# A first convolution block in 64x32 tiles, eight at once, with the large band assembled by transfers inside SBUF

## The chip, the core and the metric

The kernel runs on one core of a Trainium2 chip. The metric is the device time of one execution in microseconds; the lower, the better. The median of three runs of the kernel before is 762.4 us (761.5 to 762.61).

## The reference: what is computed

A light-weight causal convolution along the sequence, followed by a gated feed-forward layer. `x` is (8, 4096, 192), the eight heads have 24 channels each, and each head has seven taps that go through a softmax first.

```
w   = exp(weight - max); w = w / (sum(w) + 1e-9)          # weight: 8 heads x 7 taps
y   = sum over k of w[h,k] * x_pad[b, s+k, channels of h]  # six zero rows ahead of each sequence
out = (relu(y @ w_gate) * (y @ w_val)) @ w_out             # 192 -> 1536 -> 192, 32768 rows
```

## The kernel before, in words

The 32768 rows are handled as two streams of four sequences each (`st` 0 and 1), in windows of 512 rows; two windows of both streams make a unit, and there are 16 units. Engines run side by side, each with its own list of instructions in order; ACT, SP and POOL also issue DMAs, and a queue whose next DMA must wait issues nothing that stands behind it.

*The opening* (units of work before the first gate/value matmul). PE can convolve by multiplying a block of x (rows on partitions) by a band matrix: column t of head h's band holds the seven weights in rows t to t+6. The opening makes this band from the eight softmaxes and convolves the first window with it, in these steps:

- PE runs warm-up matmuls (L193), spreads the raw taps over 128 partitions (L203), and clears three PSUM regions with the matmuls of L209.
- DVE takes the maximum `mx` (L275), ACT the exponential `e` (L278) and its sum (L281), DVE makes the blocks of the band (`prod` L287, `blk` L294, `sm` L295, `blocks` L299). POOL makes `wn`, the normalised taps, from `sm` (L308).
- PE shifts the blocks into place with `Z`, a matrix of ones in one diagonal stripe: eight shifts of 16 columns for each of three groups of heads, 24 matmuls (L335). DVE casts the three results to float16 (L343): `bands`, 118 rows by 112 columns per head.
- The first window of x is loaded as five overlapping pieces `jj` (up to 118 rows, both streams side by side, 384 columns of float32, tiles `prod1` to `prod5`) by SP (pieces 0, 3, 4) and ACT (pieces 1, 2), L109, and cast to float16 by ACT (L119). `STEPS0` sets the order 1, 0, 2, 3, 4.
- `conv_steps` convolves piece by piece in 112x32 tiles of the array: four at a time, each 32 channels of one stream, 106 columns (L391). The result's three parts of channels (`c`) lie in three PSUM tiles and are cast to `xc` by ACT and DVE (L402).

*Then* `gate_val` runs the gate and value matmuls (L621) for 12 groups `f` of 128 hidden channels, ACT applies the relu (L632), DVE multiplies (L633). The second window is convolved in the same way with `conv_steps` between groups 9 and 10 (`CONV1`), the third with `conv`. All later windows are convolved outside PE, on ACT, DVE and POOL (the lanes; they use `tap`, 20 small transfers on SP, L354). The weights Wg and Wv are loaded in four portions by POOL (L224) and copied to the second half of the partitions by DVE, POOL and SP (L231). L643 projects.

The order of work is the order of the code on each engine. A DMA issued by SP or ACT counts its completion on one of eight counters (`DMAHW0` to `DMAHW7`), taken in turn over both queues. A transfer that takes a counter again waits until that counter's last transfer has landed. Counters of POOL's transfers are called `DMASW`.

Of the kernel before, what the change touches and what calls it, by code (L numbers as in the profile page):

```python
# [9 lines left out]
F16 = mybir.dt.float16  # L10
# [5 lines left out]
def kernel(  # L16
# [50 lines left out]
    const = ctx.enter_context(tc.tile_pool(name="const", bufs=1))  # L67
# [30 lines left out]
        return xt  # L98

    xts = {0: staged(0, 0).rearrange("p (j s d) -> p j s d", s=2, d=D)}  # L100
    ROWS = [SUB + PAD, 112, 112, 112, 96]
    raw = [
        apool.tile([128, 2 * LPOOL], FP, name=f"prod{jj + 1}")[:, 0 : 2 * D] for jj in range(GSUB)
    ]

    def load_raw(queue, jj):
        lo = STEP * jj - PAD
        p0 = max(0, -lo)
        queue.dma_start(  # L109
            out=raw[jj][p0 : ROWS[jj], :].rearrange("p (s d) -> p s d", s=2),  # L110
            in_=bass.AP(
                tensor=x.tensor,
                offset=x.offset + (lo + p0) * D,
                ap=[[D, ROWS[jj] - p0], [NB * S * D, 2], [1, D]],
            ),
        )

    def cast(copy, jj):
        copy(  # L119
            out=xts[0][0 : ROWS[jj], jj, :, :].rearrange("p s d -> p (s d)"),  # L120
            in_=raw[jj][0 : ROWS[jj], :],
        )

    HR = 128 // H
    BW = HR + PAD
# [1 line left out]
    nc.scalar.activation(out=early[:], in_=nc.const_aps.tensor(0.0, [128, 1], FP), func=ACTF.Exp)  # L127
    w8 = const.tile([H, KW], FP)
    nc.sync.dma_start(out=w8[:], in_=weight)
# [5 lines left out]
    nc.vector.memset(zeros[:], 0.0)  # L135
    e = const.tile([128, KW + 1], FP)
    nc.vector.memset(e[:, KW:], 1e-9)

    ones = const.tile([128, 128], FP)
    nc.gpsimd.memset(ones[:], 1.0)  # L140
# [16 lines left out]
    Z = const.tile([128, 256], F16)  # L157
# [3 lines left out]
    with nc.allow_low_precision("one of the terms is not zero"):  # L161
        nc.vector.tensor_reduce(
            out=Z[:, 112 : 112 + HR],
            in_=eye[:].rearrange("p (g i) -> p i g", i=HR),
            axis=mybir.AxisListType.X,
            op=ALU.add,
        )
# [37 lines left out]
    BANDS = [range(0, 3), range(3, 6), range(6, H)]  # L205
    raised = [psum.tile([128, 2, 512], FP, name="ps") for _ in range(2)]
    raised = [raised[0][:, 0, :], raised[1][:, 0, :], held[:, 1, :]]
    for part, heads in zip(raised, BANDS):
        nc.tensor.matmul(  # L209
            out=part[:, 0 : SUB * len(heads)],  # L210
            lhsT=zeros[:],
            rhs=none(len(heads), SUB),
            start=True,
            stop=False,
            skip_group_check=True,
        )
# [54 lines left out]
    for s in range(2):  # L271
# [4 lines left out]
        out=mx[:], in_=spread[:, 0, 0:KW], axis=mybir.AxisListType.X, op=ALU.max, negate=True  # L276
# [5 lines left out]
    for jj in STEPS0[:3]:  # L282
# [5 lines left out]
        out=prod[:],  # L288
# [8 lines left out]
    for heads in BANDS:  # L297
        n = len(heads)
        nc.vector.scalar_tensor_tensor(  # L299
            out=blocks[:, heads[0] : heads[0] + n, :],  # L300
# [8 lines left out]
        out=wn[:], in0=e[:, 0:KW], scalar1=sm[:], scalar2=None, op0=ALU.mult  # L309
# [17 lines left out]
    bands = [const.tile([128, len(heads), SUB], F16, name=f"band{heads[0]}") for heads in BANDS]  # L327
    for part, heads, to, copy in zip(
        raised, BANDS, bands, [nc.vector.tensor_copy] * 3
    ):  # L330
        n = len(heads)
        for j in range(128 // HR):
            s0 = HR * j - PAD
            lo, hi = max(0, -s0), min(BW, SUB - s0)
            nc.tensor.matmul(  # L335
                out=part[:, 0 : SUB * n].rearrange("p (h t) -> p h t", t=SUB)[:, :, s0 + lo : s0 + hi],
                lhsT=Z[:, 112 - HR * j : 240 - HR * j],
                rhs=blocks[:, heads[0] : heads[0] + n, lo:hi],
                start=False,
                stop=(j == 128 // HR - 1),  # L340
                skip_group_check=True,
            )
        copy(out=to[:].rearrange("p h t -> p (h t)"), in_=part[:, 0 : SUB * n])  # L343

    tap = const.tile([128, NCH, KW], FP)

    for c in range(NCH):
        r0 = 0
        while r0 < 64:
            h = (64 * c + r0) // G  # L350
            r1 = min(64, G * (h + 1) - 64 * c)
            row = wn[HR * h : HR * h + 8, :]
            for st in range(2):
                nc.sync.dma_start(  # L354
                    out=tap[64 * st + r0 : 64 * st + r1, c, :],
                    in_=bass.AP(
                        tensor=row.tensor,
                        offset=row.offset,
                        ap=[row.ap[0], [0, (r1 - r0) // 8], [1, KW]],
                    ),  # L360
# [4 lines left out]
            both_halves(nc.sync.dma_start, 10, Wv)  # L365

    def band(h):
        return bands[h // 3][0 : SUB + PAD, h % 3, :]

    dense, xcs = {}, {}  # L370

# [5 lines left out]
    def conv_steps(g, ps, c, steps):  # L377


        for jj in steps:  # L380
            col = STEP * jj
            n = min(STEP, WIN - col)
            rows = n + PAD
            for second in range(2):
                for st in range(2):
                    for k2 in range(2):
                        k = 2 * c + k2
                        h0, h1 = 32 * k // G, (32 * k + 31) // G
                        h, m = (h0, G * h1 - 32 * k) if second else (h1, 32)
                        p0 = 64 * st + 32 * k2  # L390
                        nc.tensor.matmul(  # L391
                            out=ps[p0 : p0 + m, 0, col : col + n],
                            lhsT=xts[g][0:rows, jj, st, 32 * k : 32 * k + m],
                            rhs=band(h)[0:rows, 0:n],
                            start=True,
                            stop=True,
                            tile_position=(0, p0),
                            skip_group_check=True,
                        )

    def evict(copy, g, ps, c):
        copy(out=dense[0][:, g, c, :], in_=ps[:, 0, :])  # L402

    def conv(g):

# [303 lines left out]
    first = [psum.tile([128, 2, 512], FP, name="ps") for _ in range(NCH)]  # L709
    for c, steps in (  # L710
        (0, STEPS0[:3]), (1, STEPS0[:3]), (0, STEPS0[3:4]), (1, STEPS0[3:4]), (0, STEPS0[4:]), (1, STEPS0[4:]), (2, STEPS0)
    ):
        conv_steps(0, first[c], c, steps)
    both_halves(nc.vector.tensor_copy, 0, Wg)
    both_halves(nc.vector.tensor_copy, 0, Wv)
    for c, copy in enumerate((nc.scalar.copy, nc.vector.tensor_copy, nc.scalar.copy)):
        evict(copy, 0, first[c], c)
# [85 lines left out]
```

## Time and profile before

| | |
|---|---|
| median of three runs | 762.4 us |
| the profiled execution, its own time | 762.03 us |
| its span, first to last instruction | 760.3 us |
| PE busy | 756.3 us (99%) |
| DVE, ACT, POOL busy | 675.5 us, 610.0 us, 461.5 us |
| first gate/value matmul starts | 7.98 us |

A row of the timeline has start, duration, engine and line, the operation with its tile names, the number of instructions merged into the row, and in brackets the idle time of that engine before the row and what ended it. `SPq`, `ACTq` and `POOLq` are the queues as they issue DMAs. "x120" means 120 instructions merged; their starts overlap, so the duration is that of the whole row. A row of the chain of work that ended last has start, duration and what.

### The profile page before, as it was taken

Reading aid. Unit: us, or ns where it says so; the run is one execution under the profiler, and the core shown is the slowest. Engines: PE = TensorE matmul, PEld = TensorE weight load, DVE = VectorE, ACT = ScalarE, POOL = GpSimd, SP = SyncE. Lnnn points to the kernel's source line nnn. Section 1 sums busy time; section 2 is a strip of 40 time slices with the busy share of each in tenths; the row PEclk is TensorE's granted clock in tenths of the full one; section 3 lists DMA queues with packets and bytes.
Section 4 is the critical chain, followed back from the end, with each engine's and each line's share of the span. In section 5 each row is a group of like instructions: output and inputs, shape, how many; then the busy total and the mean of one; then the engine's idle time right before and its main releaser. Section 6 shows DMA issues by size and latency. Waiting matters only on the chain.

```text
span 760.3 us, 30529 instructions
## 1 busy us (share of the span) xinstructions
PE 756.3 (99%) x13723; PEld 457.7 (60%) x13723; DVE 675.5 (89%) x647; ACT 610.0 (80%) x680; POOL 461.5 (61%) x311
## 2 busy tenths in 40 slices
PE   9999999999999999999999999999999999999998
PEld 5555555566666666666666666666666666666658
DVE  7889989998998989989999899998999989897891
ACT  7897887878878788887877878788797887877671
POOL 8729649195591946829377392874919659193600
PEclk9999999999999999999999999999999999999999
DMA  9953532345324443334434324352233532240302
GB/s 142 139 66 91 80 85 46 43 96 75 85 44 52 98 66 85 54 62 83 60 85 71 66 67 55 85 85 73 52 49 93 77 86 44 23 100 9 85 2 85
DMA packets 153714, 54.07 MB, mean 71 GB/s; under 512 B 148912, under 2 KB 153584, under 8 KB 153584
## 3 DMA queue, kind: packets, MB, share of 16 engines
q1 hardware_dynamic: 117152, 37.61, 21.8%
q0 software_dynamic: 35808, 14.07, 16.3%
q8 instruction: 107, 1.75, 1.0%
q10 hardware_dynamic: 624, 0.44, 0.2%
q14 instruction: 23, 0.19, 0.1%
HBM read 28.98 MB, written 25.17 MB: 71 GB/s over the span
## 4 chain that ended last, share of the span: by engine, by line
PE 99%; DVE 0%; ACT 0%; issue 0%
PE ps L621 65%; PE ps L643 31%; PE ps L686 2%; PE ps L391 0%; PE ps L193 0%; PE ps L335 0%; PE ps L414 0%; ACT xc L402 0%; PE ps L203 0%; DVE prod L287 0%; ACT out_s L697 0%; DVE blk L294 0%; DVE blocks L299 0%; ACT e L278 0%; DVE mx L275 0%
## 5 line engine op out<-in xcount | busy, mean ns | idle before, releaser
L633 DVE TENSOR_TENSOR hT<-gr,ps 128x1024 f16<-128x1024 f16 (+1 forms) x385 | 468.9, 1218 | 35.8 <-ACT gr L632 8.7
L632 ACT ACTIVATE gr<-ps 128x1024 f16<-128x1024 f32 (+1 forms) x385 | 392.8, 1021 | 114.7 <-PE ps L621 114.6
L550 POOL TENSOR_TENSOR prod<-prod,prod 128x896 f32<-128x896 f32 x145 | 302.8, 2088 | 251.3 <-DVE prod L584 242.2
L621 PE MATMUL ps<-xc,Wg 64*64 64x512 f16 (+1 forms) x4464 | 318.6, 376 | 0.2 <-ACT xc L402 0.2
L621 PE MATMUL ps<-xc,Wv 64*64 64x512 f16 (+1 forms) x4464 | 318.6, 376 | 0.0
L643 PE MATMUL ps<-hT,Wo 64*64 64x512 f16 x4320 | 235.8, 376 | 0.0
L621 PEld LDWEIGHTS <-Wv 64*64 64x64 f16 (+1 forms) x4464 | 150.0, 106 | 98.7 <-DVE hT L633 0.3
L621 PEld LDWEIGHTS <-Wg 64*64 64x64 f16 (+1 forms) x4464 | 146.6, 107 | 102.0
L643 PEld LDWEIGHTS <-Wo 64*64 64x64 f16 x4320 | 138.5, 107 | 94.4
L538 ACT ACTIVATE prod<-x_r,tap 128x1024 f32<-128x1024 f16 (+2 forms) x195 | 182.7, 1017 | 0.0
L574 DVE SCALAR_TENSOR_TENSOR acc<-x_r,tap,acc 128x1024 f32<-128x1024 f16 (+3 forms) x150 | 118.0, 853 | 0.0
L661 DVE STREAM_TRANSPOSE out_s<-ps 128x1024 f32<-128x1024 f32 x45 | 56.1, 1248 | 28.4 <-PE ps L643 24.4
L550 POOL TENSOR_TENSOR xc<-prod,prod 128x896 f16<-128x896 f32 x29 | 60.7, 2092 | 2.3
L479 POOL COPY x_p<-x_e 128x1536 f16<-128x1536 f16 (+1 forms) x32 | 42.2, 1349 | 0.0
L251 POOL DMA_DIRECT2D x_e<-in_x_dram x30 | 26.6, 890 | 0.0
L574 DVE SCALAR_TENSOR_TENSOR xc<-x_r,tap,acc 128x1024 f16<-128x1024 f16 (+3 forms) x30 | 25.2, 839 | 0.0
L563 ACT ACTIVATE acc<-x_r,tap 128x1024 f32<-128x1024 f16 (+3 forms) x30 | 22.5, 801 | 0.0
L656 ACT COPY turned_by<-ps 128x2 f32<-128x2 f32 x45 | 7.0, 154 | 16.8 <-PE ps L643 14.8
L686 PEld LDWEIGHTS <-hT 128*128 128x128 f16 x192 | 15.8, 98 | 0.4 <-issue 0.4
L686 PE MATMUL ps<-Wo,hT 128*128 128x192 f16 x192 | 16.0, 246 | 0.0
L697 ACT COPY out_s<-ps 128x768 f32<-128x768 f32 (+2 forms) x5 | 3.2, 638 | 12.7 <-PE ps L686 12.7
L697 DVE COPY out_s<-ps 128x192 f32<-128x192 f32 x1 | 0.4, 357 | 13.3 <-PE ps L686 13.3
(61 smaller groups left out, 74.6 us busy)
## 6 DMA issues: line engine op xcount, KB each, us to landing
out_dram<-out_s SPq DMA_DIRECT2D x125, 192.0 KB
x_e<-in_x_dram POOLq DMA_DIRECT2D x28, 384.0 KB, 5.8
x_r<-x_p SPq DMA_TRANSPOSE x116
prod<-in_moe_w_out_dram POOLq DMA_DIRECT2D x1, 576.0 KB, 9.1
out_dram<-out_s SPq DMA_DIRECT2D x5, 96.0 KB
out_s<-in_x_dram POOLq DMA_DIRECT2D x2, 210.0 KB, 6.2
out_s<-in_x_dram POOLq DMA_DIRECT2D x2, 192.0 KB, 6.6
x_e<-in_x_dram POOLq DMA_DIRECT2D x2, 192.0 KB, 3.8
```

Of the source, the lines that this page charges most:

```text
L251: nc.gpsimd.dma_start(out=xe[:, 0:n, st, :, :].rearrange("p j c r -> p j (c r)"), in_=bass.AP(tensor=x.tensor, offset=x.offset + row * D, ...
L479: nc.gpsimd.tensor_copy(out=xp[:, js, :, st, :], in_=xe[:, js, st, :, :])
L538: nc.scalar.activation(out=both(prods[b, k], b, at, n), in_=shifted(b, c, k, t, n), func=ACTF.Copy, scale=tap[:, c, k : k + 1],)
L550: nc.gpsimd.tensor_tensor(out=acc if k < KW - 1 else xcs[b][:, w, :, :].rearrange("p c t -> p (c t)")[:, LDVE : NCH * WIN], in0=acc, in1=p ...
L563: nc.scalar.activation(out=both(accs[b], b, at, n), in_=shifted(b, c, 0, t, n), func=ACTF.Copy, scale=tap[:, c, 0:1],)
L574: nc.vector.scalar_tensor_tensor(out=result(b, at, n) if k == KW - 1 else both(acc, b, at, n), in0=shifted(b, c, k, t, n), scalar=tap[:, c ...
L621: nc.tensor.matmul(out=pss[i][q : q + M, st, :], lhsT=W[64 * st : 64 * st + 64, c, 128 * f + q : 128 * f + q + M], rhs=xcb[64 * st : 64 * ...
L632: nc.scalar.activation(out=gr[:, sts], in_=pss[0][:, sts], func=ACTF.Relu)
L633: nc.vector.tensor_tensor(out=h[:, f, sts], in0=gr[:, sts], in1=pss[1][:, sts], op=ALU.mult)
L643: nc.tensor.matmul(out=ps[64 * st : 64 * st + 64, b, :], lhsT=Wo[64 * r : 64 * r + 64, f, p, :], rhs=hs[b][64 * r : 64 * r + 64, f, st, :] ...
L661: nc.vector.transpose(out=o[:].rearrange("p t (b d) -> p b t d", b=2)[:, :, :, 32 * p : 32 * p + 32], in_=ps[:].rearrange("p b (t c) -> p ...
L686: nc.tensor.matmul(out=ps[:, i // 2, D * (i % 2) : D * (i % 2) + D], lhsT=h[:, f, st, 128 * q : 128 * (q + 1)], rhs=Wo[:, f, :, :].rearran ...
```

## The change

The first window, and it alone, is convolved in another way. It is seen as two halves of 256 rows, half `r` on partitions 64r to 64r+63, and each half as five pieces of 58 rows (the last 24) with six rows ahead. A band of only 64 rows by 58 columns, `near`, is made; since `Z` now has its stripe twice, 64 columns apart, the matmuls put the same band on partitions 0 to 63 and 64 to 127. The shifts number four for each group of heads, 12 in all. `conv_halves` works in 64x32 tiles: eight matmuls of 58 columns, two row halves by four column positions, each half in its own PSUM bank.

The second and third window still need the large band, `large`, 118 rows by 112 columns. It is cleared by DVE and filled by two transfers on SP, which lay `near` into it twice along the diagonal.

Each of the five loads of x becomes two (rows of half 0, rows of half 1): ten loads of 64 rows, but 58 in the first half of piece 0, where six rows of padding are not loaded, and 32 and 30 in piece 4. The casts of pieces 3 and 4 are divided: stream 0 on ACT, stream 1 on DVE.

```diff
+    HALF = WIN // 2
+    PIECE = 58
...
-    ROWS = [SUB + PAD, 112, 112, 112, 96]
+    LAST = 64 + HALF - PIECE * (GSUB - 1) + PAD
+    ROWS = [64 + PIECE + PAD] * (GSUB - 1) + [LAST]
...
-    def load_raw(queue, jj):
-        lo = STEP * jj - PAD
+    def load_raw(queue, jj, r):
+        lo = HALF * r + PIECE * jj - PAD
         p0 = max(0, -lo)
+        n = min(64, -(-(ROWS[jj] - 64) // 32) * 32) if r == 0 else ROWS[jj] - 64
         queue.dma_start(
-            out=raw[jj][p0 : ROWS[jj], :].rearrange("p (s d) -> p s d", s=2),
+            out=raw[jj][64 * r + p0 : 64 * r + n, :].rearrange("p (s d) -> p s d", s=2),
...
-    for queue, steps in ((nc.scalar, (1, 2)), (nc.sync, (0, 3, 4))):
-        for jj in steps:
-            load_raw(queue, jj)
+    for queue, pieces in (
+        (nc.scalar, ((1, 0), (1, 1), (2, 0), (2, 1))),
+        (nc.sync, ((0, 0), (0, 1), (3, 0), (3, 1), (4, 0), (4, 1))),
+    ):
+        for jj, r in pieces:
+            load_raw(queue, jj, r)
...
+    large = const.tile([128, H, SUB], F16, name="large")
+    nc.vector.memset(large[:], 0.0)
+    nc.vector.memset(raw[GSUB - 1][32:64, :], 0.0)
...
+    nc.vector.tensor_copy(out=Z[:, 176 : 176 + HR], in_=Z[:, 112 : 112 + HR])
...
     for jj in STEPS0[3:]:
-        cast(nc.scalar.copy, jj)
+        cast(nc.scalar.copy, jj, slice(0, 1))
...
-        for j in range(128 // HR):
+        for j in range(64 // HR):
...
+    for jj in STEPS0[3:]:
+        cast(nc.vector.tensor_copy, jj, slice(1, 2))
+
+    for t in range(0, SUB, PIECE):
+        n = min(PIECE, SUB - t)
+        nc.sync.dma_start(out=large[t : t + n + PAD, :, t : t + n], in_=near[0 : n + PAD, :, 0:n])
...
+    def conv_halves(g, ps, c, pieces):
+        for jj in pieces:
+            col = PIECE * jj
+            n = min(PIECE, HALF - col)
+            rows = n + PAD
...
+                        for r in range(2):
+                            nc.tensor.matmul(
+                                out=ps[p0 : p0 + m, r, col : col + n],
+                                lhsT=xts[g][64 * r : 64 * r + rows, jj, st, 32 * k : 32 * k + m],
+                                rhs=near[64 * r : 64 * r + rows, h, 0:n],
+                                start=True,
+                                stop=True,
+                                tile_position=(64 * r, p0),
+                                skip_group_check=True,
+                            )
```

How this stands in the engines' lists. On ACT, from the first load of x to the third cast, before (`prod2` is the tile of piece 1, `prod1` of piece 0, `prod3` of piece 2):

```order
L109 DMA prod2_87<-in_x_dram 112x2x192
L109 DMA prod3_88<-in_x_dram 112x2x192
L278 ACTIVATE e_102<-ps_121,mx_138 128x7 [waits DVE_49]
L281 ACTIVATE total_142,sm_141<-e_102 128x8 [waits Activation_49]
L119 CAST out_s_84<-prod2_87 112x384 [waits DMAHW3_49]
L119 CAST out_s_84<-prod1_86 118x384 [waits DMAHW1_49,Pool_49]
L119 CAST out_s_84<-prod3_88 112x384 [waits DMAHW5_49]
```

and now:

```order
L113 DMA prod2_87<-in_x_dram 64x2x192 x2
L113 DMA prod3_88<-in_x_dram 64x2x192
L113 DMA prod3_88<-in_x_dram 64x2x192 [waits DMAHW1_49]
L289 ACTIVATE e_107<-ps_130,mx_147 128x7 [waits DVE_49]
L292 ACTIVATE total_151,sm_150<-e_107 128x8 [waits Activation_49]
L123 CAST out_s_84<-prod2_87 128x384 [waits DMAHW5_49,DMAHW3_49]
L123 CAST out_s_84<-prod1_86 128x384 [waits DMAHW2_49,Pool_49]
L123 CAST out_s_84<-prod3_88 128x384 [waits DMAHW7_49,DMAHW1_49]
```

There are two loads more ahead of `e`, and the second of them, which is the upper half of piece 2, carries a wait for counter 1. On SP the same place, up to the first `tap` transfer, before:

```order
L129 DMA w8_93<-in_weight_dram 8x7
L109 DMA prod1_86<-in_x_dram 112x2x192
L109 DMA prod4_89<-in_x_dram 112x2x192
L109 DMA prod5_90<-in_x_dram 96x2x192
L354 DMA tap_217<-wn_156 24x1x7 [waits Pool_49]
```

and now:

```order
L133 DMA w8_93<-in_weight_dram 8x7
L113 DMA prod1_86<-in_x_dram 58x2x192
L113 DMA prod1_86<-in_x_dram 64x2x192
L113 DMA prod4_89<-in_x_dram 64x2x192 x2
L113 DMA prod5_90<-in_x_dram 32x2x192 [waits DMAHW0_49]
L113 DMA prod5_90<-in_x_dram 30x2x192 [waits DMAHW2_49]
L360 DMA large_109<-near_196 64x8x58 [waits DMAHW3_49,DVE_49]
L360 DMA large_109<-near_196 60x8x54 [waits DMAHW4_49]
L371 DMA tap_216<-wn_165 24x1x7 [waits DMAHW5_49,Pool_49]
```

Eleven transfers are now issued on the two queues before the large band's, so the counters come round: `w` has counter 0, the first half of piece 0 (58 rows) counter 1, its second half counter 2, and the ninth to eleventh transfer take 0, 1 and 2 again. On DVE, from its first instruction to `mx`, now:

```order
L142 MEMSET zeros_105 128x64
L144 MEMSET e_107 128x1
L146 MEMSET large_109 128x448
L147 MEMSET prod5_90 32x384
L172 TENSOR_REDUCE Z_118<-eye_116 128x16 [waits Pool_49]
L178 COPY Z_118<-Z_118 128x16 [waits DVE_49]
L179 TENSOR_REDUCE mask_121<-eye_116 128x8
L189 MEMSET Wg_125 1x1
L286 TENSOR_REDUCE mx_147<-ps_130 128x1 [waits PE_49]
```

New are the two clearings ahead of `Z` and the copy behind it; before, `Z` followed the small memset of `e` directly.

More of the change, by code (lines that the diff above doesn't have):

```diff
@@ L209 @@
         nc.tensor.matmul(
-            out=part[:, 0 : SUB * len(heads)],
+            out=part[:, 0 : PIECE * len(heads)],
             lhsT=zeros[:],
-            rhs=none(len(heads), SUB),
+            rhs=none(len(heads), PIECE),
             start=True,
@@ L367, in band @@
     def band(h):
[L368 removed]
+        return large[0 : SUB + PAD, h, :]
     dense, xcs = {}, {}
@@ L402, in evict, with evict_halves @@
         copy(out=dense[0][:, g, c, :], in_=ps[:, 0, :])
+    def conv_halves(g, ps, c, pieces):
[3 more added lines that the diff above has]
+            rows = n + PAD
+            for second in range(2):
+                for st in range(2):
+                    for k2 in range(2):
+                        k = 2 * c + k2
+                        h0, h1 = 32 * k // G, (32 * k + 31) // G
+                        h, m = (h0, G * h1 - 32 * k) if second else (h1, 32)
+                        p0 = 64 * st + 32 * k2
+                        for r in range(2):
[7 more added lines that the diff above has]
+                                skip_group_check=True,
+                            )
+    def evict_halves(copy, g, ps, c):
+        copy(
+            out=dense[0][:, g, c, :].rearrange("p (r t) -> p r t", r=2), in_=ps[:, :, 0:HALF]
+        )
     def conv(g):
```

27 lines of the change are left out of this document (13 added, 14 removed).

## The prediction

> **What bounds the kernel now.** I read the page's busy times first, then the chain of work that ended last, then the opening ten microseconds of ACT, SP, DVE and POOL in the timeline, then the DMA view cut into short windows. The first two say where time can be won or lost at all:
>
> ```profile
> PE 756.3 (99%) x13723; PEld 457.7 (60%) x13723; DVE 675.5 (89%) x647; ACT 610.0 (80%) x680; POOL 461.5 (61%) x311
> ...
> PE 99%; DVE 0%; ACT 0%; issue 0%
> ```
>
> PE holds the whole chain. The chain in order of time shows its opening (start, us, what):
>
> ```profile
> 0.85 1.55 PE ps L193 x4
> ...
> 3.15 0.28 ACT e L278
> ...
> 4.23 0.30 DVE blocks L299
> ...
> 4.57 1.22 PE ps L335 x24
> 5.78 1.54 PE ps L391 x70
> ...
> 7.35 0.59 ACT xc L402
> ...
> 7.98 13.20 PE ps L621 x120
> 21.18 1.53 PE ps L391 x120
> 22.71 18.29 PE ps L621 x168
> ```
>
> From 7.98 us PE has no gap to speak of until 757: the first gate/value matmul (L621) at 7.98 is the hinge. Whatever moves it moves the end by as much, and nothing later can give that back, unless PE's own work gets longer or shorter. So the question is when L621 starts, and at what speed.
>
> Three engines lead to that point (timeline; start, us, engine and line, in brackets the idle time before and what ended it):
>
> ```profile
> 0.88 0.90 ACTq L109 DMA_DIRECT2D prod<-in_x_dram  x2
> 3.15 0.27 ACT L278 ACTIVATE e<-ps,mx 128x7 f32<-128x7 f32 x1 [0.85 <-DVE mx L275]
> 3.66 0.50 ACT L119 CAST out_s<-prod 112x384 f16<-112x384 f32 x1
> 4.75 1.75 ACT L119 CAST out_s<-prod 118x384 f16<-118x384 f32 x4 [0.60 <-DMA prod<-in_x_dram]
> 7.35 1.26 ACT L402 CAST xc<-ps 128x512 f16<-128x512 f32 x2 [0.85 <-PE ps L391]
> ...
> 0.81 0.41 SPq L129 DMA_DIRECT2D w<-in_weight_dram  x1
> 1.28 1.34 SPq L109 DMA_DIRECT2D prod<-in_x_dram  x3
> ...
> 0.89 0.11 DVE L135 MEMSET zeros<- 128x64 uint32 x1 [0.89 <-PEq L787]
> 0.95 0.06 DVE L137 MEMSET e<- 128x1 f32 x1
> 1.97 0.37 DVE L162 TENSOR_REDUCE Z<-eye 128x16 f16<-128x128 f32 x1 [0.96 <-POOL Z L158]
> ...
> 5.15 1.22 DVE L343 CAST band<-ps 128x336 f16<-128x336 f32 x3 [0.25 <-PE ps L335]
> ```
>
> ACT carries the exponential `e` at 3.15, on which DVE's `blocks` and so the band hang, and after it the five casts of x. The DMA view by windows (queue: packets, MB, share; q10 is ACT's queue, q1 is SP's) is, for 0 to 2 us, 2 to 2.5, 2.5 to 3, 0 to 6, and 7 to 15.4:
>
> ```profile
> q1 hardware_dynamic: 16, 0.00, 0.4%
> ...
> q10 hardware_dynamic: 113, 0.09, 72.8%
> ...
> q1 hardware_dynamic: 94, 0.07, 52.8%
> q10 hardware_dynamic: 122, 0.08, 49.7%
> ...
> q1 hardware_dynamic: 704, 0.49, 27.4%
> q10 hardware_dynamic: 480, 0.34, 19.8%
> ...
> q1 hardware_dynamic: 176, 0.00, 2.1%
> ```
>
> Two things are read here. SP's x loads move nothing before 2.5 us, and from then on everything moves at once. And packets count the DMA engines that a transfer uses, since each used engine adds one closing packet: the 8 rows of `w` made 8+8=16; ACT's two loads 2x112x2=448 plus 32, that is 16 each; SP's three 640, plus 48, plus the 16 of `w`, is 704; six `tap` transfers, copying 8 source rows to 24 or 16, made 128+48=176, 8 each. Every count divides the rows into equal shares: 112 and 96 by 16, 8 by 8. One packet of 768 B took 19.8% of 16 engines over 6 us, by 480, 39.6 ns.
>
> **The change part by part.**
>
> *The loads, and a wait ahead of `e`.* Five loads become ten, and SP and ACT share eight completion counters in turn, so the ninth to eleventh reuse one. In the new order ACT's fourth load (upper half of piece 2) waits for counter 1, held by SP's first, the lower half of piece 0, and `e` stands behind it on ACT. That a queue stalls as a whole is shown where SP waited for a weight load and the `tap` transfers behind went on at 16.03:
>
> ```profile
> SPq L231 <- DMA Wg<-in_moe_w_gate_dram: 3.4, 1, 3.4
> ```
>
> When does that half land? It has 58 rows, because the six padding rows are not loaded, and 58=2x29 divides equally only over 2 engines (or 1). That is 58 packets on one engine instead of 14. Bounds: spread over 16 it is 7 or 8 packets, done near 3.2; on two engines 58x39.6 ns=2.3 us from 2.55, plus up to 16 packets of ACT's other loads on these engines (0.6). I take 2.3+0.3: data at 5.15. To reach the waiting engine adds 0.3 to 0.5 (piece 0 of before: cast at 4.75; `w`, moved by 2.0, was used at 2.32); 0.4 gives 5.55. Then ACT issues for 0.45 (0.90 by two) and `e` starts at 6.0 instead of 3.15: **+2.85 us**. [...]
>
> *From `e` to the hinge.* `blocks` follows `e` by 1.08, L335 by 1.42: 7.42. L335 halves from 24 to 12 matmuls: 0.61 instead of 1.22. The three band casts shrink from 336, 336, 224 columns to 174, 174, 116: 1.22 becomes some 0.65, ending near 8.5. That saves 1.2 us of work, but now beside a longer wait: the upper half of piece 2 is issued only at 5.55. ACT's own first load was issued at 0.88, its 240 packets had moved by 3.0 (113+122, and a few before 2), so 2.5 us to use; SP's piece 0 took 3.47 (1.28 to 4.75). I take 2.8, nearer the first, since the x traffic is over by then though weight loads are not: cast of piece 2 at 8.35. Spacing of casts is 0.42 (4.75 to 6.0 for three); the ACT halves of pieces 3 and 4 cost half of that, some 0.23 spacing and 0.27 each, so they end at 9.27. SP's last load waits in the same way for the upper half of piece 0 (5.7) and lands at 8.5, no later. DVE does its two halves between 8.5 and 9.0. Then 16 last matmuls, 0.18, the eviction 0.63 (1.26 by two) and 0.04: L621 at 10.1 against 7.98. **+2.1 us**; with 2.5 and a quicker first piece +1.2, with 3.5 and 0.6 of sharing +3.2.
>
> *The convolution itself.* 120 matmuls of 106 columns, four at a time, become 240 of 58, eight at a time. Columns per stream fall to half. The timeline of before has the same 120 twice:
>
> ```profile
> 5.71 2.12 PE L391 MATMUL ps<-band,out_s 112*32 112x106 f16 x120
> ...
> 21.11 1.60 PE L391 MATMUL ps<-band,out_s 112*32 112x106 f16 x120
> ```
>
> Bounds for 240: half of 2.12, 1.1 us; or, if every matmul costs what one did (13 ns), 3.1. Most of it lies under the wait for casts, since c0 and c1 of three pieces run before; what follows the last cast is the 0.18 above (0.1 to 0.25). Worth nothing here either way.
>
> *The clock.* The page prints 1.00 throughout, but the opening ran slower: L193 streamed 3x512+128 columns in 1.55 us, 0.93 ns each, and L621 takes 13.20 us for 120, two at a time, 0.43 ns per column. The first L391 burst is the slow one of the two. So full speed came near 7 us, after PE had worked with gaps under 0.5 us from 0.85:
>
> ```profile
> 3.57 0.95 PE L209 MATMUL ps<-zeros 128*128 128x336 f16 x3
> ```
>
> Now L209 (464 columns instead of 896) ends near 4.1 and PE idles until 7.42: 3.3 us that were work. Bounds: nothing, if the speed comes at 7 regardless; or 6.1 us of work needed once more (0.85 to 7), at half speed from 10.1, 3.05 lost. From the dense stretch of before (3.57 to 7) some 3.5 us would do, 1.75 lost. I take **+1.8**. [...]
>
> *The rest.* DVE's new memsets (448 and 384 elements; 64 took 0.11) need some 0.95 us from 1.01, just inside the 0.96 it idled for POOL's `Z`; the copy inside `Z` adds under 0.1 ahead of `mx`, beside PE's work. The large band's two transfers are issued near 8.6 on SP, ahead of the `tap` transfers; L391's second burst needs them at 25. `tap` slips some 2 us on SP, about as far as everything does. POOL:
>
> ```profile
> 5.56 0.35 POOL L308 TENSOR_SCALAR wn<-e,sm 128x7 f32<-128x7 f32 x1
> 10.73 0.50 POOL L231 COPY Wg<-Wg 64x384 f16<-64x384 f16 x1 [0.53 <-DMA Wg<-in_moe_w_gate_dram]
> ```
>
> `wn` waits for `sm`, now at 7.05, and the later weight loads stand behind it: 1.5 us late, less than PE's own slip, so no new wait. PE's small stalls in its first 120 matmuls (13.20 against 120x18.29/168=13.06) vanish: -0.1.
>
> **Sum:** 2.1+1.8-0.1=+3.8 us on the profiled execution's own 762.0 (span 760.3, 1.7 around it), 765.8. The median of the runs is 762.4, 0.4 more; I put 766.0.
>
> **The rivals.**
>
> 1. *The clock is not lost.* Warm-up work before 4.1 counts, or the new convolution is enough. Same delay, no half speed: 762.0+2.0=764.0 to 764.4. For it: no row shows PE idling for 3 us once it works. Against: the slow first burst.
> 2. *58 rows spread over all engines.* 116 packets among 16 engines; the two queues together moved 216 in 0.5 us, so done by 3.2, felt at 3.65, `e` at 4.1. L621 comes 4.55 after that landing (2.8 to the cast, 0.42+0.23+0.27, 0.85): 8.2, +0.2, and a shorter gap in PE costs perhaps 0.8: 763.0. Against it: every count above is an equal division.
> 3. *Not slower.* The same spread, and the landing before 3.4, where 3.4+4.55 equals 7.98. With 3.2 and 2.5 instead of 2.8, L621 starts at 7.5 and the halved band work is gained: 761.6. SP's queue moved nothing before 2.5, so 0.9 us are left for 116 packets and the completion; possible, barely.
> 4. *Worse.* The late halves meet the weight loads and take 4 us or more, and speed comes only after 6 us: above 768.8.
>
> **How the numbers follow.** My case 0.58 (own range 764.5 to 768.5), the first rival 0.18, the second 0.16, the third 0.05, the fourth 0.03. The forecast is my case, 766.0. From 762.8 to 768.8 leaves out the third, the fourth and half of the second, 0.16. A difference of 0.2%, 1.5 us, is about what this kernel's measurement can tell from none. Slower by more: 0.55 of my case, 0.15 of the first rival, 0.02 of the second and the fourth's 0.03, 0.75. Faster by more needs 1.5 us off an opening of 8 us: 0.03. The rest, 0.22, within.
>
> **What the new profile would show.** ACT's fourth x load issued at 5 to 6 us with its queue idle before it and `e` near 6: the wait is right; `e` near 3.2: it is wrong, and so is everything built on it; near 4.1: rival 2. First cast of piece 2 released by a DMA after 8 us. L621 starting near 10; its first matmuls at 0.9 ns per column up to 13 or 14 us: the clock term. POOL's copies of weights no longer bounding PE. Wrong above all if 58 rows are not split over two engines, or if the clock does not care.

## The result and the profile after

The changed kernel takes 773.92 us (median of four runs, 772.52 to 775.46); the kernel before took 762.5 us beside it. The ratio is 1.0153, with an interval from 1.013 to 1.0176: slower by 11.4 us, where 3.6 were forecast. The profiled execution of the changed kernel has an own time of 774.55 us and a span of 772.8. Its page, busy line of PE and the shares of the chain that ended last:

```profile
PE 758.4 (98%) x13831; PEld 426.0 (55%) x13831; DVE 677.0 (88%) x652; ACT 609.8 (79%) x680; POOL 461.1 (60%) x311
...
PE 98%; DMA 1%; issue 1%; ACT 0%; SPq 0%
```

PE still holds the chain, but a DMA and "issue" (time in which the engine waited for nothing that the profile shows) are new in it, 1% each. The chain in order of time says where (start, us, what):

```profile
1.28 5.64 DMA prod<-in_x_dram
...
6.95 3.06 DMA prod<-in_x_dram
...
10.03 0.52 ACT out_s L123
...
10.59 2.06 PE ps L434 x148
12.65 3.85 issue
16.50 0.53 PE ps L434 x29
17.03 15.13 PE ps L666 x120
32.16 1.25 PE ps L408 x95
33.41 0.89 issue
...
34.78 18.24 PE ps L666 x168
```

The lines have moved: L434 is the new first convolution, L666 the gate/value matmuls (L621 before), L408 the second window's convolution (L391 before). Laid beside the chain of before, shown in the prediction, the opening loses time in four places:

| stretch | before | after | difference |
|---|---|---|---|
| start of `e` | 3.15 | 7.60 | +4.45 |
| `e` to the first gate/value matmul | 4.83 | 9.43 | +4.60 (3.85 of it "issue") |
| first 120 gate/value matmuls | 13.20 | 15.13 | +1.93 |
| second window's convolution | 1.53 | 2.62 | +1.09 (0.89 of it "issue") |
| next 168 gate/value matmuls | 18.29 | 18.24 | -0.05 |

Together 12.0 us of the 12.5 between the two executions' own times. ACT's and SP's queues show the first place (timeline; in brackets the idle time before and what ended it):

```profile
2.32 5.24 ACTq L113 DMA_DIRECT2D prod<-in_x_dram  x2
7.60 0.27 ACT L289 ACTIVATE e<-ps,mx 128x7 f32<-128x7 f32 x1 [5.30 <-DMA prod<-in_x_dram]
...
10.03 1.02 ACT L123 CAST out_s<-prod 128x384 f16<-128x384 f32 x3 [1.02 <-DMA prod<-in_x_dram]
```

`e` stands 5.3 us behind a load: the wait is the one forecast, but the half it waits for lands at 6.93 instead of 5.55. PE shows the second place:

```profile
9.79 0.39 PE L434 MATMUL ps<-near,out_s 64*32 64x58 f16 x32
10.59 2.06 PE L434 MATMUL ps<-near,out_s 64*32 64x58 f16 x167 [0.41 <-ACT out_s L123]
16.50 0.53 PE L434 MATMUL ps<-near,out_s 64*32 64x58 f16 x41 [3.85 <-issue]
```

All data is there, the same line goes on before and after, and yet PE stands still for 3.85 us with 41 of its 240 matmuls left. The queue `q8` of the DMA view, called "instruction", brings one packet of 0.02 MB at a time. In the kernel before, one arrived in the first 10 us; in the changed one none, and one between 10 and 15 us (queue: packets, MB, share). Before, 0 to 10 us:

```profile
q8 instruction: 1, 0.02, 0.6%
```

and after, 10 to 15 us (q0 is GpSimd's queue):

```profile
q0 software_dynamic: 607, 0.57, 80.2%
...
q8 instruction: 1, 0.02, 2.3%
```

That packet moved from 13.37 to 15.24 us, and PE went on at 16.50. So the question for the experiments was whether PE had run out of instructions, and if so why the packet came so late.

### The profile page after: what moved, and what is told of

Its sections match the earlier page's. It is cut to its first block, busy times and chain, and to the rows that moved or that the text cites. A ratio compares the mean times of both kernels' runs of the same rounds, so it can differ in the third digit from the quotient of the medians.

```text
span 772.8 us, 30767 instructions
## 1 busy us (share of the span) xinstructions
PE 758.4 (98%) x13831; PEld 426.0 (55%) x13831; DVE 677.0 (88%) x652; ACT 609.8 (79%) x680; POOL 461.1 (60%) x311
## 4 chain that ended last, share of the span: by engine, by line
PE 98%; DMA 1%; issue 1%; ACT 0%; SPq 0%
PE ps L666 65%; PE ps L688 30%; PE ps L731 2%; DMA prod<-in_x_dram 1%; PE ps L434 0%; PE ps L408 0%; PE ps L459 0%; ACT out_s L123 0%; SPq L133 0%; ACT out_s L742 0%
## 5 line engine op out<-in xcount | busy, mean ns | idle before, releaser
L666 PE MATMUL ps<-xc,Wg 64*64 64x512 f16 (+1 forms) x4464 | 315.6, 377 | 0.0
L666 PE MATMUL ps<-xc,Wv 64*64 64x512 f16 (+1 forms) x4464 | 315.1, 376 | 0.0
L666 PEld LDWEIGHTS <-Wv 64*64 64x64 f16 (+1 forms) x4464 | 143.8, 106 | 105.8 <-issue 1.4
L666 PEld LDWEIGHTS <-Wg 64*64 64x64 f16 (+1 forms) x4464 | 133.5, 107 | 115.9 <-issue 1.4
L688 PEld LDWEIGHTS <-Wo 64*64 64x64 f16 x4320 | 126.3, 107 | 106.7
```

The source lines that it names most:

```text
L666: nc.tensor.matmul(out=pss[i][q : q + M, st, :], lhsT=W[64 * st : 64 * st + 64, c, 128 * f + q : 128 * f + q + M], rhs=xcb[64 * st : 64 * ...
L688: nc.tensor.matmul(out=ps[64 * st : 64 * st + 64, b, :], lhsT=Wo[64 * r : 64 * r + 64, f, p, :], rhs=hs[b][64 * r : 64 * r + 64, f, st, :] ...
```

## The experiments

Each edit is on the changed kernel unless another is named. "Listed instructions" are the weight loads and matmuls in PE's list: 43 stand ahead of the first convolution in the changed kernel (21 matmuls with a weight load each, and the float32 matmul of the taps, which is listed once and shown by the trace as two pairs), and each of the convolution's 240 matmuls has a weight load of its own, so it uses 480.

### The loads: e1_other_queue and e2_48_rows

The first takes the waiting load from ACT and gives it to SP:

```diff
-        (nc.scalar, ((1, 0), (1, 1), (2, 0), (2, 1))),
-        (nc.sync, ((0, 0), (0, 1), (3, 0), (3, 1), (4, 0), (4, 1))),
+        (nc.scalar, ((1, 0), (1, 1), (2, 0))),
+        (nc.sync, ((0, 0), (0, 1), (2, 1), (3, 0), (3, 1), (4, 0), (4, 1))),
```

> Edit: the upper half of piece 2 is loaded by SP (third of its x loads) instead of ACT, so that ACT issues three loads and none of them waits; on SP the loads of piece 4 now wait for counters 1 and 2. Theory (the wait ahead of e is the first term, worth 4.45 us): e starts near 3.2 us instead of 7.6, the band is ready before 6, and the first convolution waits for piece 0's slow half alone, near 7; the first gate/value matmul comes at 10 to 13, the time falls by 3 to 6 us against the changed kernel. Rival (the slow half of piece 0 is what counts, whoever waits for it): e is early but the first gate/value matmul stays within 1 us of 17.0 and so does the time.

772.93 us, ratio 1.0133 [1.0109, 1.0156]. `e` is back at 3.15, yet the median is only one microsecond lower, inside the spread of the two kernels' runs: now SP's queue stalls on the same slow half, and its last load arrives late (timeline of ACT):

```profile
11.04 0.35 ACT L123 CAST out_s<-prod 94x192 f16<-94x192 f32 x1 [2.53 <-DMA prod<-in_x_dram]
```

and its chain has the gap again:

```profile
12.26 2.77 issue
```

The first gate/value matmul starts at 15.56, between what the theory and the rival said, and the 3 to 6 us of the theory did not come. So the wait ahead of `e` alone isn't worth the 4.45 us by which `e` moved; the slow half holds up whichever queue waits for its counter. The second run loads 48 rows of that half instead of 58 (it leaves ten rows of x out), since 48, like the 112 and 96 of the prediction's counts, makes equal shares for 16 engines:

```diff
-        p0 = max(0, -lo)
+        p0 = 16 if lo < 0 else 0
```

> Edit: the lower half of piece 0 loads 48 rows instead of 58; the first ten rows of each stream are taken as zero, so ten rows at the start of the output are left out of the computation. Nothing else moves; ACT's fourth load still waits for this half. Theory (58 rows go over two DMA engines, 48 over sixteen): the half lands near 3.7 to 4.3, ACT's fourth load is issued there, e starts at 4.2 to 4.8 instead of 7.6, and the time falls by about 3 us. Rival (the half is late because ten loads share the bandwidth, or because of its place in the queue): e stays at 7.0 to 7.6 and the time does not move.

773.39 us, ratio 1.0144 [1.0123, 1.0165]. Timeline:

```profile
4.91 0.27 ACT L289 ACTIVATE e<-ps,mx 128x7 f32<-128x7 f32 x1 [2.60 <-DMA prod<-in_x_dram]
```

and the chain:

```profile
8.88 2.11 PE ps L434 x134
10.98 5.63 issue
...
17.14 14.39 PE ps L666 x120
```

Ten rows fewer make the half land at 4.24 instead of 6.93. In the runs that load 58 rows in the same place (the changed kernel, e1, e3, e4, g2) it landed between 6.82 and 8.09. The changed kernel's own packets say the same, counted as in the prediction. Its DMA view from 0 to 10 us has for SP's queue

```profile
q1 hardware_dynamic: 721, 0.48, 19.3%
```

and 721 is 16 for `w`, 3x144 for the loads of 64 rows, 80 and 75 for those of 32 and 30, and 116+2 for the 58 rows; over 16 engines these would have made 116+16, 735 in all. So 58 rows went over two engines. But the time fell by 0.5 us, inside the spread, not by the 3 expected: the main part of the convolution starts 1.7 us sooner (8.88 against 10.59), stands still for 5.63 us instead of 3.85, and the gate/value matmuls start where they did. What the loads win here, the gap takes.

### The gap: e3_half_matmuls and g1_doubled_before

If PE runs out of instructions, fewer of them make no gap. This run leaves out the second matmul of each pair of heads, half of the 240 (the lower head's channels keep the upper head's taps):

```diff
-            for second in range(2):
+            for second in range(1):
```

> Edit: in the first window's convolution the second matmul of each pair (the channels of the lower head in each group of 32) is left out, 120 matmuls in 64x32 tiles instead of 240; those channels get the wrong head's taps. Theory (PE's list ran dry at 12.65 us, because the instructions of the new convolution are used up faster than the next 16 KB of them arrive): with 240 instructions fewer the idle 3.85 us inside the convolution is gone, the first gate/value matmul starts near 12.5 to 13 and the time falls by 3.5 to 5 us. Rival (a change of tile size or of PSUM bank drains PE, or a wait that the profile does not show): the gap stays at 3 to 4 us in the convolution or just behind it, and the time falls by under 1.5 us.

769.68 us, ratio 1.0093 [1.0073, 1.0113], 4.2 less than the changed kernel. Both gaps are gone from the chain, as the theory said, though `e` was later in this execution (8.76):

```profile
12.08 0.79 PE ps L434 x53
...
13.53 14.91 PE ps L666 x120
28.44 1.58 PE ps L408 x120
```

The counterpart leaves the kernel before as it is, with its old tiles and loads, and does each piece of its first convolution twice:

```diff
-        conv_steps(0, first[c], c, steps)
+        conv_steps(0, first[c], c, [s for s in steps for _ in range(2)])
```

> Edit, to the kernel before: every matmul of the first window's convolution is issued twice (240 in the old 112x32 tiles, four at a time; the second writes the same result). No load, band or tile size changes. Theory (PE's first 445 instructions are there from the start, the next 256 come as one 16 KB transfer that is asked for on the way): PE idles inside this convolution too, at its 445th instruction, but for 2 us or less, since that transfer is asked for at 6.9 us and moved at 8.3 to 9.2 as before; the first gate/value matmul starts at 10 to 12 instead of 7.98. Rival (the idle stretch belongs to the small tiles or to the two PSUM banks): no gap, 120 matmuls more cost 1.3 to 2.1 us, the first gate/value matmul starts at 9.3 to 10.

765.59 us, ratio 1.0043 [1.0028, 1.0058]. The gap appears in the old tiles, with the old loads, and is 2.41 us long where 2 or less were expected (timeline; L391 is the old convolution, 67 listed instructions stand ahead of it):

```profile
5.71 2.74 PE L391 MATMUL ps<-band,out_s 112*32 112x106 f16 x188
10.87 0.75 PE L391 MATMUL ps<-band,out_s 112*16 112x106 f16 x52 [2.41 <-issue]
```

That excludes the 64x32 tiles, the PSUM banks, the new band and the ten loads as its cause. And the place agrees: 67+2x188=443 listed instructions here, 43+2x199=441 in the changed kernel. The gap comes at a count of instructions, not at a place in the work.

### The clock: e4_keep_warm

Ten matmuls of 512 columns fill PE's idle time ahead of the band:

```diff
+    hold(*[4] * 10)
```

> Edit: ten matmuls of 512 columns on constants are put between the clearing of the PSUM regions and the shifts of the band, where PE idles from 4.15 to 9.0 us; they write a region that nobody reads. Theory (the slow clock costs 2 us because PE idled): the first 120 gate/value matmuls take 13.0 to 13.4 us instead of 15.13, at 0.43 ns per column from their start; the time falls by about 2 us; the idle stretch inside the convolution stays. Rival (the full clock comes at a time of its own, near 21 us): the first gate/value matmuls stay at 0.8 ns per column and the time does not move.

772.56 us, ratio 1.0136 [1.0114, 1.0158]; about 2 us were expected, and the 1.4 that came lie inside the spread of the two kernels' runs. The windows of PE (from:to, length, busy (instructions), granted clock, DMA share, GB/s):

```profile
7.00:9.00 2.00, 0.04 (x1) 1.00 0.58 86
9.00:13.00 4.00, 2.50 (x201) 0.90 0.64 106
13.00:17.00 4.00, 0.28 (x39) 0.50 1.13 158
...
23.00:25.00 2.00, 2.00 (x22) 1.00 1.35 156
```

The clock was lost at 12.17 in spite of the filling (the mean of 0.90 from 9 to 13 is 0.83 us at half), and stayed at half for 10.2 us. That is 0.86 us ahead of the gap, which began at 13.03; ahead of it PE had idled from 7.04 to 9.69 and from 10.70 to 11.45. So this loss is not the gap's, and the run doesn't say what the gap alone does to the clock. 120 gate/value matmuls took 15.55 us, no less than the 15.13 of the changed kernel. The gap came after 189 matmuls of the convolution instead of 199: the ten fillers are 20 listed instructions, and 63+2x189 is 441 again.

### Why the packet is late: g2_no_large_transfers, g3_loads_mended, g4_loads_and_instructions

First suspect: the two transfers that assemble `large`, issued at 10.20. The run leaves them out (the second and third window are convolved with a band that isn't filled):

```diff
-    for t in range(0, SUB, PIECE):
-        n = min(PIECE, SUB - t)
-        nc.sync.dma_start(out=large[t : t + n + PAD, :, t : t + n], in_=near[0 : n + PAD, :, 0:n])
```

> Edit, to the changed kernel: the two transfers that fill the large band are left out, so the second and third window are convolved with a band of zeros. Theory (the 992 runs of 116 or 108 bytes of these two transfers stand in the way of the instruction transfer, which began 3.0 to 6.9 us after the first of them was issued in every run so far): the instruction transfer begins within 1.5 us of PE's 189th instruction instead of 2.2 to 5.2, the gap shrinks from 3.85 to 1 to 2 us, and the time falls by 2 to 3 us; the second gap, of 0.89 at the second window, may shrink too. Rival (the weight loads stand in its way, or it always takes this long): the gap stays at 3 to 5 us.

772.88 us, ratio 1.0137 [1.012, 1.0154]; the gap is still 3.64 us. These two transfers inside SBUF are not what delays the packet, and that theory fell.

Then the loads were mended: nine of x instead of ten, pieces 1 to 3 of a half and a stream in one transfer, and the 58 rows as 48 and 10.

```diff
+    load_three(nc.scalar, 0, 0)
+    load_three(nc.scalar, 0, 1)
+    load_three(nc.scalar, 1, 0)
+    load_three(nc.sync, 1, 1)
+    load_rows(nc.sync, 0, 0, PAD, 48)
+    load_rows(nc.sync, 0, 1, 0, 64)
+    load_rows(nc.sync, 0, 0, PAD + 48, 10)
...
```

> Edit, to the changed kernel: pieces 1 to 3 are loaded by half and stream, three pieces in one transfer of 64 rows, piece 0's lower half as 48 and 10 rows; nine loads, none of which has 58 rows or stands ahead of e with a wait for a late load. Theory: e near 3.2 to 3.7, all casts done by 7.5, PE reaches its 445th instruction by 8.5 and then idles until the instruction transfer has come, at 10 to 16 as in the runs before; so the time falls by no more than the idle stretch lets it, to 766 to 772. Rival (the late loads were the whole loss, the gap only a cover for something else): the first gate/value matmul at 8 to 9.5 and a time of 762 to 764.

772.52 us, ratio 1.0133 [1.0117, 1.0148]. `e` is at 3.15 and the casts are done at 8.72, yet the time is outside the 766 to 772 expected, and far from the rival's 762 to 764 (chain; L443 and L675 are the convolution and the gate/value matmuls of this kernel):

```profile
8.26 2.07 PE ps L443 x151
10.34 4.41 issue
...
15.27 15.88 PE ps L675 x120
```

The main part of the convolution starts 2.3 us sooner than in the changed kernel (8.26 against 10.59). The gap takes 0.56 of it, and the first 120 gate/value matmuls take 0.75: their pairs follow each other every 0.43 us from 15.20 to about 21.0, in the changed kernel from 16.96 to about 21.2.

The next run adds 164 listed instructions ahead of all this, by cutting the warm-up into small matmuls, so that PE passes the place 256 ahead of the dry point sooner:

```diff
-    WARM = [(4, 4, 4, 1), (4, 3)]
+    WARM = [(4, 4, 4, 1), (4, 4, 1)]
...
-        for reps in counts:
+        for _ in range(4 * sum(counts)):
...
-                out=held[:, 0, 0 : 128 * reps],
-                lhsT=many(128),
-                rhs=many(128 * reps),
+                out=held[0:32, 0, 0:32],
+                lhsT=many(32),
+                rhs=many(32),
```

> Edit, to the kernel of g3: the warm-up matmuls on constants are cut into pieces of 32 by 32 (88 instead of 6), which moves every later PE instruction back by 164, so that the point where the next 256 are asked for comes before the convolution and the next dry point (701) behind it. Theory: no idle stretch of over 1 us inside the convolution; if one comes, it is at the 701st instruction, 5 to 20 instructions into the gate/value matmuls; the time is 1 to 4 us under g3's. Rival (the gap does not depend on the count of PE instructions): it stays where it was in the convolution and as long.

772.34 us, ratio 1.0133 [1.0118, 1.0149]: the place is as the theory said, but the 1 to 4 us under g3 did not come. The convolution has no gap any more; it comes five matmuls into the gate/value stage:

```profile
11.11 1.39 PE ps L675 x5
12.50 2.91 issue
```

207 listed instructions ahead of the convolution, 480 in it, 10 for five gate/value matmuls: 697, which is 441+256. So PE runs dry after 441, or after 697 where the next 256 came in time. The packets have that size too: in h4 below, q8 moved 109 packets and 1.79 MB in all, 16.4 KB each, 64 bytes for each of 256.

### Supply, clock and traffic: h1_supply_and_clock, h2_all_three, h3_late_weights, h4_all_four

The first puts 205 small matmuls and six large ones ahead of `near`, so that the convolution starts with its instructions fetched; the loads stay as changed:

```diff
+    small(205)
+    hold(*[4] * 6)
     near = const.tile([128, H, PIECE], F16, name="near")
```

> The changed kernel with 205 matmuls of 32 by 32 (410 of TensorE's instructions) and then six of 512 columns, all on a scratch bank, put in TensorE's idle time ahead of the products of `near`; the loads are as in the change. The first convolution then begins at instruction 469 instead of 43, so that the piece of instructions that it runs out of has long been fetched, and the one after it is asked for before it begins. Theory (supply of instructions, and the clock lost by idling): no idle time in the middle of the convolution, first gate/value matmul at 14.0 to 14.5 instead of 16.96, the first 120 of them in 13.2 to 13.7 instead of 15.13 because TensorE is busy from 0.9 on; 768.5 to 770.5 us. Rival (the dry point only moves on, as when 164 instructions were put in): idle time of 2 us or more shortly after the convolution's end, 771.5 or more.

776.96 us, ratio 1.0196 [1.0181, 1.0212]: slower still, and the rival was right. The gap moves on (timeline; L442 is the convolution, L674 the gate/value matmuls):

```profile
13.80 1.52 PE L442 MATMUL ps<-near,out_s 64*32 64x58 f16 x124 [1.33 <-issue]
...
21.37 0.61 PE L674 MATMUL ps<-xc,Wg 64*128 64x512 f16 x2 [5.08 <-issue]
```

With 465 listed instructions ahead (the expectation says 469, which counts four too many, as do the 445, 701 and 957 of others), the dry points are 465+2x116=697 and, after the other 124 matmuls and four of the gate/value stage, 953. The supply for the second moved from 19.04 to 19.98, 5.24 us after PE had gone on past 697 at 13.80.

h2 takes the mended loads and puts 120 small matmuls in place of the warm-up, 90 behind the products of `near`, and two larger ones (512 and 256 columns, where the expectation says three of 512):

> As the run before, and the first block's loads mended (nine transfers, all spread over the DMA engines): 120 small matmuls instead of the warm-up, 90 more behind the products of `near`, three of 512 columns. Convolution from about 8 to 12.3, first gate/value matmul at 12.3 where the kernel before has 7.98; if the clock is kept as well, the rest is as before. Theory: 762.3 + 4.3 = 766.6, between 765 and 768: what is left is the convolution's own 240 matmuls and the casts' later data. Rival (the instructions run dry in another place): 770 or more, with a gap of 2 us or more.

773.28 us, ratio 1.0154 [1.0132, 1.0176]; 766.6 was expected, and the rival was right. The gap is in the convolution, at 455+2x121=697 (chain; L452):

```profile
10.79 3.34 issue
14.13 1.35 PE ps L452 x111
```

h3 asks what makes the supply late. It is the kernel with the mended loads and two fills on GpSimd ahead of the weight loads, so that these move after the convolution:

```diff
+    pool_halves(2)
+    nc.gpsimd.memset(Wg[64:128, :, 384:1280], 0.0)
+    nc.gpsimd.memset(Wv[64:128, :, 384:1280], 0.0)
     for s in range(2, 4):
         load_w(s)
-    pool_halves(2)
```

> The kernel with the nine mended loads, and GpSimd given two fills of some microseconds ahead of the weight loads of columns 384 on and of the second block's x, so that these transfers start after the convolution (the fills write what is overwritten later). Theory A (the fetch of instructions is late because the DMA engines are full of weight transfers): the packet of instructions, asked for near 8.5 us, starts before 10.5 instead of 12.24, and the gap of 4.41 falls under 2.5. Theory B (the fetch takes its 3 us whatever else is under way): the packet and the gap stay as they were, within 0.7 us. The total is not what is looked at; the weights may come late for the gate/value matmuls.

One run, 769.91 us (762 before). The queues from 8.5 to 12.2 us, with the mended loads alone:

```profile
q0 software_dynamic: 572, 0.55, 101.7%
```

and with the late weights:

```profile
q8 instruction: 1, 0.02, 2.3%
q0 software_dynamic: 6, 0.00, 0.5%
```

and PE in the same kernel (timeline; L445 is the convolution):

```profile
12.27 0.53 PE L445 MATMUL ps<-near,out_s 64*32 64x58 f16 x41 [1.79 <-issue]
```

With GpSimd's queue q0 full, no packet of instructions moved in this stretch; with it empty, the packet moved from 9.43 to 10.77 instead of 12.24 to 13.21, and the gap fell from 4.41 to 1.79. Theory A holds in this one execution. PE had passed the place 256 instructions ahead of the dry point at the same time in both, 8.53 and 8.57.

h4 joins all of it, h2 with late weights:

> The mended loads, the small matmuls ahead of the convolution (so that it begins at instruction 457 and the clock is kept) and the late weights of the run before, with fills of about 3.8 us instead of 4.6. Theory (three terms: loads, supply of instructions held up by the weight transfers, clock): the convolution runs from about 9.4 to 13.3 with under 1 us of idle time in it, the gate/value matmuls start near 13.3 where the kernel before has 7.98, at full clock, and all behind is as before: 762 + 5.3 = 767.3, between 766 and 768.5. Rival (the fetch takes 3 us and more on an idle queue too): a gap of 2 us or more at instruction 701 or 957, and 769 or more.

770.89 us, ratio 1.0111 [1.0094, 1.0128]; 767.3 was expected, 769 or more by the rival. What was left (chain; L454 is the convolution, L686 the gate/value matmuls):

```profile
10.45 1.76 issue
...
13.71 15.69 PE ps L686 x120
```

and PE in that gap (columns of the windows as in e4):

```profile
10.50:12.20 1.70, 0.00 (x0) 0.91 0.02 1
```

The DMA engines were idle in that window (share 0.02), and PE still waited 1.76 us. So the rival keeps a part: the fetch takes 3.65 us with the weight loads out of the way too (the place 256 ahead passed at 8.56, packet 9.57 to 10.94, PE on at 12.21). 1.45 us into that pause, at 11.9, the clock fell to half and stayed there to 18.7: 15.69 us for 120 matmuls instead of 13.20. None of these kernels beats the one before.

## Why the prediction was wrong

*The wait ahead of `e`.* Right in its mechanism: ACT's fourth load waits for counter 1, held by 58 rows on two engines (116+2 packets), and `e` stands behind it (5.3 us, and 2.69 less with 48 rows). The term was mis-sized: 6.93 in place of 5.55 for the landing and 7.60 in place of 6.0 for `e`. Two things were left too small: an issue by ACT took 0.60 to 0.72 us, not 0.45, and some 1.4 us of landing (6.93 against 5.55) is beyond "58 packets and up to 16 others"; what those two engines carried besides was not measured apart.

*From `e` to the hinge.* The casts came nearly as said: the last of ACT's ends at 11.05, 3.45 after `e`, against 3.27 forecast. Of the hinge's 9.05 us of delay (2.1 forecast) the step's own working explains little; the rest is the next point.

*The convolution itself.* "Worth nothing here either way" is the step that failed, twice over. First, only 32 of the 240 matmuls lay under the wait for the casts: the piece that comes late, piece 2, is the third of c0 in PE's list, it was missing until 10.55, and what stands behind it on PE, c1 and c2 of the early pieces too, waited with it. So 2.06+0.53=2.6 us of matmuls came after that cast, 2.1 of them after the last cast (11.05 to 12.65 and 16.50 to 17.03), where the prediction has 0.18 and then an eviction of 0.63. This needed no run to be seen: the prediction itself has piece 2 as the late one. At 2.06 us for 167, 12.3 ns each, the matmuls cost about what they cost before (13), near the upper bound of 3.1 for all 240. Second and larger, 3.85 us, the supply of instructions, which has no term in the prediction. One line of the view from 7 to 15.4 us that it quotes, which it leaves out, could have asked the question:

```profile
q8 instruction: 2, 0.03, 1.6%
```

The new convolution spends 480 instructions instead of 240. In the kernel before, PE reached the place 256 ahead of the end of its supply at 6.93, the packet moved from 8.29 to 9.23, and PE would have been dry only at 15.17, since the gate/value matmuls use up instructions slowly (120 of them, 240 listed instructions, in 13.20 us). In the changed kernel 256 instructions last 128x12.3 ns=1.6 us, while from PE's passing the place 256 ahead to its going on 5.6 us went by (10.90 to 16.50). The shortest such time at a gap is 3.35 us (h1's first, 10.45 to 13.80), then 3.65 (h4) and 3.74 (h3).

*The clock.* Right in size: +1.8 forecast, +1.93 measured for the first 120 gate/value matmuls, and half speed until about 21 us, later than the 13 or 14 forecast. Half speed is read here from the spacing of 0.43 us between pairs: the windows of the changed kernel print a granted clock of 1.00 from 15 to 20 us, those of e4 0.50 from 17 to 21, with the same spacing. That some 3.5 us of dense work bring the full speed was the author's estimate from one stretch of the kernel before, and no run shows it; the stretches at half that were measured lasted 6.8 us (h4) and 10.2 us (e4). The gap of 3.85 us, which was not forecast, stands ahead of these matmuls too, but e3, which has no gap, still needs 14.91 us for them, +1.71. The rival that the clock is not lost is excluded by the changed kernel itself: its first gate/value pairs follow each other every 0.43 us where the kernel before has 0.21. Nor does full speed come at a time of its own: that spacing ends near 17.2 in e3 and near 21.2 in the changed kernel.

*The rest.* The clearings on DVE fit; the large band's transfers and `tap` are hidden (g2 without the former is 1.0 us less in its median, inside the two runs' spread); GpSimd's late `wn` ends no wait of PE, but the weight loads behind it now fill the DMA engines during the fetch (q0 94.1% from 10.9 to 16.4 us). What was not foreseen is the second gap of 0.89 us in the second window's convolution. It comes after 43+480+240+2x95=953 instructions, which is 441+2x256, and vanishes in e3, where the count shifts. So it is the same supply.

*The sum.* Of the 7.9 us between 766.0 and 773.92, 1.6 are the later `e` and 0.2 the casts; the last cast to L666 took 5.98 (11.05 to 17.03) instead of 0.85, of which 3.85 are the first gap and 1.3 the matmuls left behind the casts; 1.1 are the second convolution and 0.1 the clock. Together 8.15. Rivals 2 and 3 fell with the landing. Rival 4 gave the right side of 768.8 by another mechanism, which is luck: the later `e` and the casts are 1.8 of the 7.9 us, 767.8 by the sum, and with mended loads the time stays at 772.52.

*What stays open.* Why the packet starts 1.4 us after PE has passed the place 256 ahead in the kernel before, with the weight loads just as busy, 2.5 us after in the changed kernel and 3.7 to 5.2 us in others (g3, h1, e2), is not settled; h3 shows that the traffic matters, not which part of it.

## What to carry to other kernels

Splitting the matmuls into smaller tiles doubled PE's instructions here (480 in the convolution instead of 240), and the burst of short ones was bounded by their supply: 256 lasted 1.6 us and their fetch 3.35 us or more. Before such a split, count the list's weight loads and matmuls from the start and look where q8's packets fall. Spreading a burst over work that uses instructions slowly would follow from this, but no run here tried it. A gap marked "issue" in the middle of one line, with all data there, is the sign to look for; what arrives sooner ahead of it can make it longer by as much, as in e2.

## What was not expected of the hardware

- PE has about 441 listed instructions at its start, and then gets 256 at a time: the twelve kernels shown with a gap (all but e3 and the one before) stopped after 441 (443 in g1), 697 or 953. Later gaps in the traces of g4, h1 and h4 (at 34.55, 39.60 and 33.92 us) come after 1209 and 1465, again 256 apart.
- From the packet's end to PE's next matmul 1.3 to 1.7 us passed (15.24 to 16.50 at the first gap and 32.64 to 34.30 at the second of the changed kernel, 10.77 to 12.27 in h3, 10.94 to 12.21 in h4).
- The granted clock fell to 0.50 some 1.45 us into a pause, for 6.8 us (h4), and in e4 after idle stretches of 2.65 and 0.75 us, for 10.2 us.
